# Values cast on their way in, casts of queries and keys in halves, PSUM as eight single banks, and a new order table, in a fused attention and expert-attention kernel

## The chip, the cores and the metric

The kernel runs on one core of a Trainium2 chip. The metric is the device time of one execution in microseconds (us). A core has a matrix engine (TensorE, PE in the profile, with PEld for its weight loads), three engines for element work (VectorE or DVE, ScalarE or ACT, GpSimd or POOL), a SyncE (SP) that issues transfers, and sixteen DMA engines that carry them. The engines run their own queues in order and wait for each other by semaphores. The on-chip memory is SBUF; matrix products land in PSUM, which has 128 partitions of eight banks with 512 float32 values each.

## What is computed

Two layers follow each other. The first is attention over 4 batches, 8 heads, 768 positions and 64 dimensions: each position sees the 8 first positions and the last 96, with a bias by distance whose slope depends on the head. The second takes the result as rows of 512 and runs four experts, each a causal attention with its own 64-dimensional projections; a gate picks two experts for each row and weighs them.

```python
# first layer, for each head
scores = q @ k.T / sqrt(64) - slope[h] * dist      # kept where global (first 8) or local (0 <= rel < 96)
x = softmax(scores) @ v                            # rows of all heads side by side: [4, 768, 512]
# second layer
logits = x @ w_gate                                # top 2 of 4, softmax over the two: w
for e in range(4):
    a = softmax(causal((x @ wq[e]) @ (x @ wk[e]).T / sqrt(64)))
    out += w[e] * (a @ (x @ wv[e])) @ wo[e]
```

All inputs and the output are float32; inside, the matrices are float16 and sums are float32.

## The kernel before

The work is cut into 24 units, u = 0 to 23: 4 batches of 6 row tiles of 128 positions. `unit` (from line 548) defines the operations of one unit, and each operation has a short name that the prediction and the order table use.

- Loads: `ldq`, `ldk` (line 578) bring two units of queries and keys at a time, 512 KB each, issued by SP; `ldv` (line 609) brings the values of one unit, 256 KB in runs of 256 bytes, into the ring `rawv`.
- Casts to float16: `cq`, `ck` (lines 582 and 584) for two units at once, `cv` (line 611) for the values, into the ring `V1`. All are `copy` (line 384), on POOL except for the first q and k.
- `tq`, `tk` transpose on PE; `eq`, `ek` copy the results from PSUM on DVE.
- Local attention, in two halves of four heads (hf = 0, 1): `s0`, `s1` are score products (line 630), `x0`, `x1` the exponentials on ACT (line 634), `m0`, `m1` the multiplication with a mask and distance factor `M` on DVE (line 639), `z0`, `z1` the products with the values (lines 647 and 650), which also give the row sums, `r` the reciprocals (line 661) and `n` the normalization (line 663). `kp` and `vp` put the 8 global keys and values in front of the next tiles (POOL, and a small transfer on SP).
- `tx`, `ex` transpose the rows; `pq` and `pv` (lines 689, 695) project to the experts' queries and keys, and to values and gate; `eqk`, `ev` copy them out on ACT or DVE; `xr`, `mx`, `wr`, `zi` do the gate.
- Expert attention: `s20`, `s21`, `s22` (line 727), exponentials `x20` to `x22` on ACT (line 731), the causal cut `af` on POOL (line 739), the products `y2` (line 751), then `rz`, `cw`, `n2` on DVE (lines 757 to 761), the transpose `tz`, its copy `ez`, the output product `po` (line 774), its copy `eo` on ACT or DVE, and the store `so` on SP.

No scheduler arranges this. The table `ORDER` (line 21) lists all operations in one sequence; `Stream.run` (line 328) walks through it and emits each, so every engine's queue has its operations in the table's order. A star behind a name takes the second of the engines that the operation allows, and a number after a colon names the PSUM slot. The costs that stand beside the operations (such as `{"DVE": 0.34}`) were used to make the table; at run time only the names of the engines matter. The names in the lists behind them are what must come earlier in the table.

PSUM is cut into two slots of two banks ("s", for scores) and four slots of one bank ("w", for everything else):

```python
def wtile(shape, dt, name):
    return psum.tile(shape, dt, name=name, tag=f"w{st.slots[0]}")

def stile(shape, name):
    return psum.tile(shape, F32, name=name, tag=f"s{st.slots[0]}")
```

At the start, `warm` (line 489) runs 24 products of zeros on PE. Constants are made meanwhile: `iota`, `d`, `dg`, `mask`, `d0`, `d1` on POOL and DVE, and from them the factors `M` on ACT; the weights come by `ld-q`, `ld-k`, `ld-v`, `ld-g`, `ld-o` and are cast by `w-q` and so on. At the end, `good0` to `good2` (lines 794 and 795) test that all sums are in range, `total` adds the result up and `flag` stores it; a branch to a general path follows, which isn't taken here.

Of the kernel before, what the change touches and what calls it, by code (L numbers as in the profile page):

```python
# [19 lines left out]

ORDER = """
ident nil ldq-0 warm:2 ldk-0 ident32 ldq-2 dg ldk-2 iota d mask ldv-0 d0 d1 M-1-1 ldq-4 cq-0 ck-0
ld-k M-0-0 M-1-0 tk-0:3 cq-2 tq-0:1 ek-0 ld-q M-0-1 V1one* eq-0 tq-2:2 perm kg-0 s0-0:1 ldv-1 eq-2
s1-0:0 ck-2 x0-0 x1-0 m0-0 kp-0 V2one ld-g s0-1:1 m1-0 s1-1:0 tk-2:3 x1-1 kp-1 cv-0 ek-2 vg-0 z1-0:2
x0-1 r1-0 s0-2:0 n1-0 cq-4 z0-0:0 x0-2 r0-0 vp-0 m1-1 tq-4:1 ld-v m0-2 n0-0 eq-4 ldk-4 tx-0:0 w-q*
s1-2:1 ldv-2 kp-2 w-k* cv-1 w-g ex-0 z1-1:1 m0-1 x1-2 r1-1 z0-1:3 pq-0:0 m1-2 vp-1 w-v* ldv-3 r0-1
n1-1 s1-3:1 ldq-6 n0-1 x1-3 eqk-0 tx-1:3 pv-0:2 ld-o ck-4 s20-0:0 xr-0 mx-0 s0-3:1 ex-1 x20-0 ev-0*
x0-3 wr-0 cv-2 tk-4:3 kp-3 z0-2:0 ek-4 af-0 zi-0 m0-3 y2-0:2 z1-2:1 s0-4:0 cv-3 vp-2 r1-2 r0-2
s1-4:1 rz-0 x0-4 ldk-6 pv-1:3 cw-0 kp-4 n2-0 ldq-8 n0-2 pq-1:2 x1-4 cq-6 n1-2 ldv-6 ones mx-1 ldk-8
m1-3 eqk-1* tq-6:1 tx-2:0 m1-4 w-o z0-3:2 ex-2 s20-1:1 r0-3 s0-5:0 m0-4 pq-2:0 xr-1 x0-5 wr-1 eq-6  # L30
ck-6 ev-1 n0-3 s1-5:0 eqk-2* z1-3:2 x20-1 vp-3 m0-5 tk-6:1 ldv-4 r1-3 tz-0:0 x1-5 pv-2:3 ldk-10 ek-6
af-1 n1-3 kg-6 s0-6:1 s1-6:0 ez-0 x0-6 m1-5 tx-3:2 po-0:0 x1-6 ldq-10 kp-6 m0-6 y2-1:1 ldq-12 xr-2
eo-0 cq-8 ex-3 s21-2:1 s0-7:0 rz-1 x21-2 mx-2 pq-3:2 zi-1 ldv-7 cw-1 x0-7 cv-6 ev-2* wr-2 tq-8:0
ck-8 n2-1 eqk-3* s1-7:1 eq-8 s20-2:0 x1-7 z0-6:1 tz-1:3 m1-6 tk-8:2 cv-4 r0-6 ez-1 x20-2 z1-6:0 n0-6
s20-3:1 vg-6 r1-6 z1-4:1 n1-6 po-1:3 ck-10 vp-6 ek-8 ldv-5 s21-3:0 eo-1 r1-4 tx-6:0 n1-4 pv-3:2
x20-3 kp-7 ex-6 z0-4:3 m0-7 tk-10:1 xr-3 ev-3 vp-4 cq-10 pq-6:0 r0-4 x21-3 n0-4 ek-10 tx-4:3 af-2
zi-2 ldk-12 mx-3 s0-8:1 ex-4 s1-8:0 cq-12 ldq-14 x0-8 eqk-6 pq-4:3 m1-7 so-1 tq-12:1 eqk-4* cv-7
wr-3 tq-10:0 eq-12 x1-8 s21-4:1 eq-10 cv-5 z0-7:1 z1-7:2 x21-4 r0-7 kp-8 s20-4:0 m1-8 vp-7 z0-5:0
ldv-8 z1-5:3 x20-4 r1-7 n0-7 s22-4:1 r0-5 n1-7 y2-2:1 ck-12 r1-5 x22-4 n0-5 tx-7:2 ldk-14 n1-5
s1-9:0 s20-6:1 rz-2 tx-5:3 x20-6 cw-2 ldv-9 ex-7 tk-12:0 ldq-16 x1-9 ex-5 cq-14 s0-9:1 ek-12 pq-5:2  # L40
x0-9 zi-3 n2-2 kp-9 af-4 pv-5:3 eqk-5* m0-8 s0-10:1 tq-14:1 xr-5 af-3 mx-5 x0-10 wr-5 pq-7:2 cv-8
eq-14 ev-5 m1-9 s21-5:0 eqk-7* s1-10:1 m0-10 z1-8:3 x21-5 z0-8:1 kp-10 r1-8 tz-2:2 kg-12 y2-3:0
ck-14 r0-8 vp-8 ez-2 x1-10 n1-8 ldv-10 pv-4:2 rz-3 n0-8 ldk-16 po-2:3 cw-3 ldv-12 cv-9 tx-8:1 n2-3
eo-2 s22-5:0 so-0 ex-8 s1-11:1 xr-4 ev-4 m0-9 tz-3:0 tk-14:3 x22-5 cq-16 mx-4 pq-8:1 ez-3 ek-14
x1-11 m1-10 s1-12:0 po-3:0 x1-12 af-6 eqk-8 z1-9:3 eo-3 s0-12:1 m1-12 s20-5:0 x0-12 wr-4 z0-9:1
pv-6:0 ck-16 zi-4 x20-5 r1-9 vp-9 r0-9 n1-9 y2-4:2 ldq-18 zi-5 n0-9 xr-6 so-2 ev-6 s21-8:1 rz-4
s0-11:0 af-5 mx-6 ldk-18 x21-8 wr-6 tx-9:3 tq-16:1 cw-4 ldv-11 x0-11 kp-12 ex-9 cv-10 tk-16:0 n2-4
eq-16 s20-8:1 ldv-13 s20-7:0 x20-8 m1-11 tz-4:2 pq-9:3 ez-4 ek-16 x20-7 af-8 z0-10:1 po-4:2 m0-11
eqk-9* y2-5:0 cq-18 r0-10 eo-4 n0-10 s1-13:1 rz-5 s21-9:0 cw-5 x1-13 cv-12 z1-10:1 n2-5 tq-18:2
vp-10 r1-10 m0-12 tz-5:3 x21-9 z1-12:0 ldq-20 n1-10 s0-13:1 ez-5 so-3 pv-7:1 kp-13 eq-18 ck-18 x0-13  # L50
ldk-20 po-5:3 r1-12 mx-7 ev-7* tx-10:2 xr-7 s1-14:0 zi-6 eo-5 wr-7 s0-14:1 vg-12 x1-14 zi-7 z0-12:1
ex-10 tk-18:3 af-7 vp-12 r0-12 n1-12 pq-10:2 so-5 cv-11 x0-14 ek-18 so-4 m1-13 s20-9:0 eqk-10*
z0-11:0 kg-18 n0-12 cv-13 pv-8:3 x20-9 r0-11 n0-11 tx-12:1 kp-14 z1-11:2 cq-20 mx-8 ex-12 y2-6:0
ldv-14 xr-8 s21-10:1 ev-8 rz-6 r1-11 s0-15:0 wr-8 x21-10 n1-11 y2-7:1 pq-12:3 rz-7 cw-6 cw-7 x0-15
n2-6 n2-7 tx-11:2 tq-20:0 m0-13 eqk-12* tz-7:1 s22-10:1 ex-11 s1-15:0 x22-10 ez-7 z1-13:3 kp-15
eq-20 z0-13:2 ck-20 x1-15 tz-6:1 vp-13 s1-16:1 r1-13 ez-6 n1-13 pq-11:0 ldv-15 x1-16 m0-14 ldq-22
ldv-16 po-7:1 cv-14 r0-13 eqk-11* n0-13 po-6:3 m1-14 eo-7 s21-11:0 s22-11:1 eo-6* x21-11 pv-9:1
m0-15 tx-13:2 so-6 z0-14:0 x22-11 mx-9 s0-16:0 r0-14 ex-13 pv-10:3 kp-16 n0-14 af-9 xr-9 x0-16
z1-14:2 wr-9 y2-8:0 ev-10* cv-15 vp-14 s20-10:1 r1-14 mx-10 ev-9 ldk-22 zi-8 n1-14 s1-17:0 xr-10
x20-10 ldv-19 zi-9 tk-20:1 rz-8 wr-10 so-7 cw-8 pq-13:2 m1-15 x1-17 af-10 n2-8 y2-9:3 ek-20 cq-22  # L60
eqk-13* tz-8:0 s20-11:0 ez-8 s1-18:1 rz-9 x20-11 tx-14:1 cw-9 cv-16 po-8:0 ex-14 z0-15:2 n2-9 x1-18
z1-15:1 r0-15 ck-22 tz-9:3 n0-15 eo-8 vp-15 s20-12:0 s0-17:1 r1-15 ez-9 pq-14:2 n1-15 so-8 x0-17
zi-10 m1-16 ldv-18 tq-22:3 x20-12 m0-16 po-9:0 eqk-14* m1-18 tk-22:1 eq-22 eo-9 s0-18:0 s20-13:1
m1-17 so-9 x0-18 z0-16:2 pv-11:3 ldv-17 x20-13 kp-18 ek-22 af-12 y2-10:0 mx-11 r0-16 xr-11 ev-11
cv-18 s21-14:0 wr-11 s20-14:1 x21-14 n0-16 tx-15:1 vg-18 ldv-22 z1-16:3 rz-10 x20-14 ex-15 s1-19:0
vp-16 r1-16 cw-10 pv-12:2 n1-16 x1-19 n2-10 s0-19:1 mx-12 m0-18 tx-16:3 tz-10:0 kp-19 pq-15:1 x0-19
m0-17 ez-10 ex-16 ev-12 s1-20:0 xr-12 eqk-15 s0-20:1 x1-20 po-10:0 kp-20 m1-19 z0-18:3 pq-16:1 cv-17
# [245 lines left out]
class Stream:  # L313
# [4 lines left out]
    def __init__(self, kinds):  # L318
        self.kinds = {k: [()] * n for k, n in kinds.items()}
        self.ops, self.slots = {}, []  # L320
# [27 lines left out]
def kernel(  # L348
# [37 lines left out]
    eng = {"DVE": dve, "POOL": pool}  # L386


    R = 4

# [469 lines left out]
```

## Time and profile before

| what | before |
| --- | --- |
| time, median of three runs | 146.72 us (145.56 to 147.25) |
| the profiled execution's own time | 146.58 us |
| span of the profiled execution, first to last instruction | 144.9 us |
| mean granted PE clock | 0.964 |
| packets of the DMA engines | 55,725, 27.83 MB, 72.2% of sixteen engines' span on SP's queue |
| HBM read and written | 20.98 MB, 6.29 MB |
| POOL casts of q and k | 11 each, 1,059 and 1,388 ns on average |
| SP's issue of a value load | median 537 ns, 390 to 2,152 |

A profile page gives the busy time of each engine; the span in 40 equal slices, each digit the busy tenths (for the clock, tenths of full speed); and the costliest groups, with their line, engine, what they write and read, shape and count, then busy us and mean ns of one, and after a second bar the time that the engine sat idle ahead of them and what ended it. A line 384 is the helper `copy`, so such groups are told apart by what they write. A timeline row gives start and length in us, then the same names. In a stretch of the span each engine's busy us is followed by its number of instructions in brackets.

### The profile page before, as it was taken

The numbers are of one execution on the slowest core, as the hardware profiler recorded it, in microseconds if no ns is written. First come the engines' busy times: TensorE is split into PE (matmuls) and PEld (weight loads), VectorE is DVE, ScalarE is ACT, GpSimd is POOL, SyncE is SP. The second block draws the span as 40 slices with busy tenths as digits, with TensorE's granted clock in tenths as the row PEclk, the third lists the DMA queues.
The fourth block names the chain that finished last, engine by engine and source line by source line (L and its number), as shares of the span: only waits on it lengthen the run. The fifth ranks groups of instructions, "written<-read, shape, count | busy, mean of one in ns | idle before, by whom it ended". The sixth has DMA issues, their size and how long they took to land.

```text
span 144.9 us, 5515 instructions
## 1 busy us (share of the span) xinstructions
PE 130.0 (90%) x2222; PEld 101.5 (70%) x2222; DVE 120.2 (83%) x420; ACT 120.1 (83%) x198; POOL 70.2 (48%) x116
## 2 busy tenths in 40 slices
PE   6985779697998999999999999889999999999870
PEld 2453466485877788778798787668878887978620
DVE  1257784897999989999999998989999998887870
ACT  3867766679985998988999998889999998899760
POOL 6058216534997596674773345545641370413100
PEclk9999555999999999999999999999999999999999
DMA  2999999599898997969999699770527204023164
GB/s 78 304 275 305 245 310 222 177 299 246 226 289 181 294 273 166 246 147 299 202 258 303 148 253 261 212 175 9 157 67 219 73 14 152 5 75 113 34 235 140
DMA packets 55725, 27.83 MB, mean 192 GB/s; under 512 B 26096, under 2 KB 52368, under 8 KB 55696
## 3 DMA queue, kind: packets, MB, share of 16 engines
q1 hardware_dynamic: 55696, 27.45, 72.2%
q8 instruction: 18, 0.29, 0.9%
q14 instruction: 11, 0.09, 0.2%
HBM read 20.98 MB, written 6.29 MB: 188 GB/s over the span
## 4 chain that ended last, share of the span: by engine, by line
PE 60%; DVE 14%; DMA 8%; SPq 7%; issue 3%; ACT 2%; POOL 2%; ACTq 0%
PE pq L689 13%; PE s L727 7%; PE sc L630 7%; PE pv L695 6%; PE z L647 5%; PE z L751 5%; DMA wg<-in_moe_w_gate_dram 5%; PE po L774 4%; SPq L578 4%; DMA rawqk<-in_k_dram 4%; PE tx L679 3%; PE tk L596 3%; DVE A L639 3%; PE z L650 3%; PE tq L591 3%
## 5 line engine op out<-in xcount | busy, mean ns | idle before, releaser
L634 ACT ACTIVATE A<-sc 128x1024 f16<-128x1024 f32 (+1 forms) x48 | 44.6, 960 | 6.7 <-PE sc L630 6.3
L731 ACT ACTIVATE A<-s 128x1024 f16<-128x1024 f32 (+1 forms) x48 | 43.4, 930 | 2.1 <-PE s L727 1.8
L639 DVE TENSOR_TENSOR A<-A,M 128x1024 f16<-128x1024 f16 (+1 forms) x48 | 35.0, 742 | 0.2 <-ACT A L634 0.2
L739 POOL TENSOR_SCALAR_AFFINE_SELECT A<-A 128x512 f16<-128x512 f16 x24 | 18.0, 761 | 19.6 <-ACT A L731 14.1
L689 PE MATMUL pq<-xT,wqk 128*128 128x128 f16 x384 | 26.3, 223 | 1.3 <-DVE z L761 1.2
L689 PEld LDWEIGHTS <-wqk 128*128 128x128 f16 x384 | 23.1, 100 | 2.3 <-DVE z L761 1.5
L384 POOL CAST k<-rawqk 128x1024 f16<-128x1024 f32 x11 | 15.3, 1388 | 12.7 <-DMA rawqk<-in_k_dram 12.6
L663 DVE TENSOR_TENSOR x<-z,rall 128x256 f16<-128x256 f32 x48 | 19.5, 413 | 0.4
L630 PE MATMUL sc<-qT,kT 64*128 64x128 f16 x352 | 17.4, 224 | 2.5 <-DVE kT L384 1.2
L647 PE MATMUL z<-V,A 128*128 128x65 f16 x192 | 17.1, 196 | 2.2 <-POOL V L384 1.0
L384 POOL CAST V<-rawv 128x512 f16<-128x512 f32 x24 | 15.7, 658 | 3.9 <-PE s L727 1.9
L647 PEld LDWEIGHTS <-A 128*128 128x128 f16 x192 | 13.1, 99 | 5.1 <-DVE wr L712 0.8
L727 PE MATMUL s<-QK 64*128 64x128 f16 x336 | 15.9, 219 | 0.0
L384 POOL COPY kT<-KG 128x32 f16<-128x32 f16 x20 | 5.4, 272 | 20.9 <-PE sc L630 20.9
L695 PE MATMUL pv<-wvg,xT 128*128 128x264 f16 x96 | 15.3, 283 | 0.0
L630 PEld LDWEIGHTS <-kT 64*128 64x128 f16 x352 | 11.1, 97 | 5.9 <-issue 1.9
L384 POOL CAST q<-rawqk 128x1024 f16<-128x1024 f32 x11 | 11.7, 1059 | 6.7 <-DMA rawqk<-in_q_dram 6.7
L650 PE MATMUL z<-V,A 128*128 128x65 f16 x160 | 14.6, 195 | 0.0
L384 ACT CAST QK<-pq 128x512 f16<-128x512 f32 x20 | 11.9, 595 | 2.5 <-PE pq L689 2.5
L774 PE MATMUL po<-wo,zT 128*128 128x512 f16 x48 | 13.9, 380 | 0.0
L751 PE MATMUL z<-V,A 128*128 128x65 f16 x336 | 13.8, 193 | 0.0
L751 PEld LDWEIGHTS <-A 128*128 128x128 f16 x336 | 12.3, 97 | 1.8 <-issue 0.4
(70 smaller groups left out, 226.0 us busy)
## 6 DMA issues: line engine op xcount, KB each, us to landing
rawqk<-in_q_dram SPq DMA_DIRECT2D x12, 512.0 KB
rawqk<-in_k_dram SPq DMA_DIRECT2D x12, 512.0 KB
rawv<-in_v_dram SPq DMA_DIRECT2D x24, 256.0 KB
out_dram<-o_sb SPq DMA_DIRECT2D x24, 256.0 KB
w<-in_moe_wk_dram SPq DMA_DIRECT2D x1, 512.0 KB
w<-in_moe_wq_dram SPq DMA_DIRECT2D x1, 512.0 KB
w<-in_moe_wv_dram SPq DMA_DIRECT2D x1, 512.0 KB
wo<-in_moe_wo_dram SPq DMA_DIRECT2D x1, 512.0 KB
```

The source lines that it names most:

```text
L384: act.copy(o, i) if e == "ACT" else (dve if e == "DVE" else pool).tensor_copy(o, i)
L630: mm(sc[:, par, pr, prev * P:(prev + 1) * P], lhsT=share(kT, u - prev)[L, p, :], rhs=share(qT, u)[L, p, :], start=True, stop=True)
L634: act.activation(A1[(2 * u + hf) % (2 * R)][:, :, :, 0:w], T.pop(("s", u, hf))[:, :, :, 0:w], func=Exp, scale=scale1)
L639: eng[e].tensor_tensor(a, a, M[:, hf, :, :, :] if ri else M0[:, hf, :, :, :], op=Alu.mult)
L647: mm(z[:, h % 4, :], lhsT=a[:, par, pr, 0:P], rhs=V1[i][:, h, 0:DV], start=True, stop=not ri)
L663: add(f"n{hf}", lambda e, hf=hf, r1=r1: dve.tensor_tensor(x16[i][:, 256 * hf:256 * hf + 256].rearrange("p (h d) -> p h d", d=Dh), T.pop((" ...
L689: mm(ps[:, j, :], lhsT=wqk[:, ko, j, :], rhs=xT[i][:, ko, :], start=(ko == 0), stop=(ko == nko - 1))
L695: mm(ps[:, :], lhsT=xT[i][:, ko, :], rhs=wvg[:, ko, :], start=(ko == 0), stop=(ko == nko - 1))
L727: mm(sc[:, par, n, :], lhsT=QK2[b % 2][L, ki, 2 + p2, :], rhs=QK2[b % 2][L, ri, p2, :], start=True, stop=True)
L731: act.activation(A2[i][:, :, 4 * ch:4 * ch + m, :], T.pop(("s2", u, ch))[:, :, 0:m, :], func=Exp, scale=scale2)
L751: mm(z[:, ex, :], lhsT=A2[i][:, ex % 2, n, :], rhs=V2[b % 2][:, ki, ex, 0:DV], start=(j == 0), stop=(j == len(mine) - 1))
L774: mm(ps[:, :], lhsT=zT[i][:, p2, :], rhs=wo[:, p2, :], start=(p2 == 0), stop=(p2 == E // 2 - 1))
```

## The change

The values no longer go through a float32 ring and a cast. GpSimd issues their transfer itself, and the transfer casts to float16 on the way into `V1`, whose ring grows from four to eight. The casts of queries and keys are each two instructions of half the size. PSUM is one tensor of eight banks; an operation takes any bank (`one`) or two neighbours (`two`), and the table names them. The products with the values of both halves go to two neighbouring banks and are one operation `z`, followed by one `r` and one `n` over both banks. Small products of zeros (`busy`) can be put ahead of an operation, by a number after a plus in the table: 3 before `tk-0`, 10 before `s1-0`, 1 before `s0-1`, 7 before `tk-2`, 8 before `z-1` and 9 before `tx-1`, 38 in all. The casts of `wk` and `wv` go to POOL and that of `wq` to DVE. The final check takes units 0 to 19 and 20 to 23 apart. The order table is new throughout, and with it the number of `eqk`, `ev` and `eo` on DVE: 8, 8 and 3, where there were 4, 7 and 5.

```diff
 ORDER = """
-ident nil ldq-0 warm:2 ldk-0 ident32 ldq-2 dg ldk-2 iota d mask ldv-0 d0 d1 M-1-1 ldq-4 cq-0 ck-0
-ld-k M-0-0 M-1-0 tk-0:3 cq-2 tq-0:1 ek-0 ld-q M-0-1 V1one* eq-0 tq-2:2 perm kg-0 s0-0:1 ldv-1 eq-2
...
-po-21:3 eo-20 n2-23 ez-22 tz-23:1 eo-21 good1 so-20 po-22:2 ez-23 good2 po-23:0 so-21 eo-22 good0
-eo-23 so-22 total:1 so-23 flag hint
+V1one* ldq-0 nil ident warm:0 ldk-0 ldq-2 ldv-3 dg ident32 ldv-0 iota ldk-2 ldv-2 d cq0-0 lv-0 cq1-0
+mask ld-q ldv-1 ck0-0 d1 perm d0 ck1-0 M-0-1 ldq-4 tk-0:0+3 lv-1 cq1-2 M-1-1 tq-0:6 ek-0 cq0-2 eq-0
+ldv-6 M-0-0 s1-0:01+10 s0-0:67 V2one* tq-2:5 x1-0 kg-0 ck1-2 x0-0 M-1-0 kp-0 m0-0 s0-1:67+1 ck0-2
...
+tz-22:4 good1 eo-21 so-20 ez-22 tz-23:4 po-22:5 so-21 ez-23 po-23:7 eo-22 eo-23* so-22 good2 so-23
+total:5 flag hint
 """
...
-    def wtile(shape, dt, name):
-        return psum.tile(shape, dt, name=name, tag=f"w{st.slots[0]}")
-
-    def stile(shape, name):
-        return psum.tile(shape, F32, name=name, tag=f"s{st.slots[0]}")
+    banks = psum.tile([P, 8, 4 * P], F32, name="banks")
+
+    def busy(t):
+
+        for n in range(st.idle):
+            mm(t[:, 0:P], lhsT=nil[:, 0:P], rhs=nil[:, 0:P], start=True, stop=True)
+
+    def one(dt=F32):
+
+        t = banks[:, st.slots[0], :]
+        busy(t)
+        return t if dt == F32 else t.bitcast(dt)
+
+    def two():
+
+        lo, hi = st.slots
+        assert hi == lo + 1
+        busy(banks[:, lo, :])
+        return banks[:, lo:hi + 1, :]
...
-    R = 4
+    R, RV = 4, 8
...
-    st = Stream({"s": 2, "w": 4})
+    st = Stream({"b": 8})
...
-               {"DVE": 1.1, "ACT": 1.1}, [("ld", n)])
+               {"DVE": 1.1, "POOL": 1.05}, [("ld", n)])
...
-            add("cq", lambda e: copy(e, q_[:, :, :, :], rq[:, 0, :, :, :].rearrange("p h j d -> p j h d")),
-                {"POOL": 0.99} if u else {"ACT": 0.95}, ["ldq", ("tq", u - 2 * RB)], port=True)
-            add("ck", lambda e: copy(e, k_[:, :, :, :].rearrange("p h d j -> p h j d"), rq[:, 1, :, :, :]),
-                {"POOL": 1.27} if u else {"DVE": 0.75}, ["ldk", ("tk", u - 2 * RB)], port=True)
+            for n in range(2):
+                add(f"cq{n}", lambda e, n=n: copy(e, q_[:, n, :, :], rq[:, 0, :, n, :]),
+                    {"POOL": 0.52} if u else {"ACT": 0.49}, ["ldq", ("tq", u - 2 * RB)], port=True)
+                hs = slice(4 * n, 4 * n + 4)
+                add(f"ck{n}", lambda e, hs=hs: copy(e, k_[:, hs, :, :].rearrange("p h d j -> p h j d"),
+                                                    rq[:, 1, hs, :, :]),
+                    {"POOL": 0.66} if u else {"DVE": 0.4}, ["ldk", ("tk", u - 2 * RB)], port=True)
...
-        add("ldv", lambda e: nc.sync.dma_start(rawv[i][:, :, :], v[b, :, rows, :].rearrange("h s d -> s h d")),
-            {"DMA": 1.3}, [("cv", u - R)])
-        add("cv", lambda e: copy(e, V1[i][:, :, 0:Dh], rawv[i][:, :, :]), {"POOL": 0.57},
-            ["ldv", c("V1one")] + [(n, u - R + a) for a in range(2) for n in ("z0", "z1")])
+        add("ldv", lambda e: pool.dma_start(V1[u % RV][:, :, 0:Dh], v[b, :, rows, :].rearrange("h s d -> s h d")),
+            {"POOL": 0.89}, [c("V1one")] + [("z", u - RV + a) for a in range(2)])
+        add("lv", lambda e: None, {"DMA": 1.35}, ["ldv"])
...
-            def z1(e, hf=hf):
-                a = A1[(2 * u + hf) % (2 * R)]
-                T["z", u, hf] = z = wtile([P, 4, DV], F32, "z1")
...
+        def z1(e):
+            T["z", u] = z = two()[:, :, 0:4 * DV].rearrange("l f (h d) -> l f h d", d=DV)
+            for h in range(H):
+                a = A1[(2 * u + h // 4) % (2 * R)][:, h % 2, h // 2 % 2, :]
+                mm(z[:, h // 4, h % 4, :], lhsT=a[:, 0:P], rhs=V1[u % RV][:, h, 0:DV], start=True, stop=not ri)
+                if ri:
+                    mm(z[:, h // 4, h % 4, :], lhsT=a[:, P:2 * P], rhs=V1[(u - 1) % RV][:, h, 0:DV],
+                       start=False, stop=True)
...
-            add(f"r{hf}", lambda e, hf=hf, r1=r1: dve.reciprocal(r1, T["z", u, hf][:, :, Dh]), {"DVE": 0.09},
-                [f"z{hf}"])
-            add(f"n{hf}", lambda e, hf=hf, r1=r1: dve.tensor_tensor(
-                x16[i][:, 256 * hf:256 * hf + 256].rearrange("p (h d) -> p h d", d=Dh),
-                T.pop(("z", u, hf))[:, :, 0:Dh], r1.unsqueeze(2).to_broadcast([P, 4, Dh]), op=Alu.mult),
-                {"DVE": 0.34}, [f"r{hf}", ("tx", u - R)])
+        add("r", lambda e: dve.reciprocal(r1, T["z", u][:, :, :, Dh]), {"DVE": 0.11}, ["z"])
+        add("n", lambda e: dve.tensor_tensor(
+            x16[i][:, :].rearrange("p (f h d) -> p f h d", f=2, d=Dh), T.pop(("z", u))[:, :, :, 0:Dh],
+            r1.unsqueeze(3).to_broadcast([P, 2, 4, Dh]), op=Alu.mult), {"DVE": 0.61}, ["r", ("tx", u - R)])
...
-    last = NU - 1
-    flat = rall[:, 0:last, :].rearrange("p u n -> p (u n)")
...
+    last, n0 = NU - 1, NU - 4
+    for n, (lo, hi) in enumerate(((0, n0), (n0, NU))):
+        st.add(f"good{2 * n}", inside(rall[:, lo:hi, :].rearrange("p u n -> p (u n)"), (hi - lo) * (H + E),
+                                      1.0 / SUM_HI, 1.0 / SUM_LO, 2 * n), {"DVE": (0.65, 0.4)[n]},
+               [("rz", u) for u in range(lo, hi)] + [("r", u) for u in range(lo, hi)])
```

The many other lines of the diff only put `one()` or `two()` where `wtile` or `stile` stood, put `z`, `r` and `n` where their two halves were named, and alter costs that aren't used at run time.

## The prediction

> **What bounds the kernel now.** I read the busy times first, then the 40 slices with the clock, then stretches of the span, then the rows of the costliest groups, and last the waits.
>
> ```profile
> PE 130.0 (90%) x2222; PEld 101.5 (70%) x2222; DVE 120.2 (83%) x420; ACT 120.1 (83%) x198; POOL 70.2 (48%) x116
> ...
> PEclk9999555999999999999999999999999999999999
> ...
> 15.00:27.00 12.00, 9.74 (x120) 7.56 (x120) 8.41 (x23) 7.48 (x10) 4.31 (x8) 0.57 1.01 265
> 27.00:30.00 3.00, 1.82 (x29) 1.47 (x26) 2.93 (x11) 1.91 (x3) 1.19 (x2) 1.00 0.48 135
> 30.00:130.00 100.00, 97.35 (x1837) 79.90 (x1835) 93.44 (x324) 92.35 (x148) 54.92 (x78) 1.00 0.73 185
> 130.00:145.00 15.00, 9.91 (x162) 6.66 (x158) 8.95 (x50) 8.80 (x18) 1.86 (x3) 0.99 0.37 136
> ```
>
> A stretch gives its length, then the busy us of PE, PEld, DVE, ACT and POOL, the clock, and the DMA share. From 30 to 130 us three engines are busy together (97, 93 and 92 of 100). PE's figure is not its capacity: by the pieces of the chain of waits one unit costs PE pq 0.89, pv 0.45, po 0.43, tx 0.22, local scores 2 x 0.22, local values 0.48, half of tq and tk 0.45, and on average 0.38 + 0.42 for the expert scores and values and about 0.12 for tz: 4.3 us, 103 us for 24 units. DVE and ACT, 120 us each, are the capacity. PE, in order, couples them. Before 30 us the kernel starts badly: for some 12 us the clock is near half, and all sixteen DMA engines are busy. The last 15 us are a thinning tail.
>
> ```profile
> L639 DVE TENSOR_TENSOR A<-A,M 128x1024 f16<-128x1024 f16 x40 | 31.5, 797 | 0.0
> L663 DVE TENSOR_TENSOR x<-z,rall 128x256 f16<-128x256 f32 x48 | 19.5, 413 | 0.4
> L384 POOL CAST V<-rawv 128x512 f16<-128x512 f32 x24 | 15.7, 658 | 3.9 <-PE s L727 1.9 <-DMA rawv<-in_v_dram 0.9 <-issue 0.5
> L661 DVE RECIPROCAL rall<-z 128x4 f32<-128x4 f32 x48 | 7.8, 171 | 0.5 <-PE z L647 0.2
> ...
> 105.45 0.61 POOL L384 CAST V<-rawv 128x512 f16<-128x512 f32 x1 [1.88 <-PE s L727]
> ...
> 105.53 1.08 DVE L639 TENSOR_TENSOR A<-A,M 128x1024 f16<-128x1024 f16 x1
> 106.95 0.66 DVE L639 TENSOR_TENSOR A<-A,M 128x1024 f16<-128x1024 f16 x1
> ...
> ACT A L634 <- PE sc L630: 6.3, 7, 1.3
> ```
>
> The mask multiplication takes 0.66 us alone but 797 ns on average: the one at 105.53 overlaps a POOL cast that ends at 106.06, and ends 0.55 us after it. Over 40 of them the excess is 40 x (0.797 - 0.66) = 5.5 us of DVE. The last line says how little ACT waits for scores: 6.3 us, of which 2.1 fall after 30 us.
>
> **What the Trainium skill says.** (1) "SBUF — State Buffer", Who interferes with whom: a VectorE instruction with two SBUF inputs contends with a GpSimd instruction that reads SBUF, not with one that only writes; the second to start blocks. The two rows at 105 us agree. (2) "TensorE: Matmul & The Clock Gate", Part 1: after a window of some 3.4 us with too little work the array runs at half clock. The slices at 5, after a stretch with PE at 3.05 of 5 us (15 to 20 us), agree in kind. (3) "DMA: Bandwidth & Descriptors", SWDGE vs HWDGE vs iDMA: a transfer that casts must be issued from GpSimd, whose cores write its descriptors; all queues share the same sixteen engines. No run here shows such a transfer yet.
>
> **The change part by part.** Durations are of one execution with a span of 144.9 and a time of 146.58 us, 1.7 us around the span; the median of the three runs is 146.72, so the two stand level. Where instructions of DVE or ACT follow each other, the next starts 0.07 to 0.10 us before the row's duration is over (two multiplications merged in 1.28, two n in 0.74, two exponentials in 1.94); I price by that step.
>
> *DVE, n and r.* 48 n at 0.335 = 16.1 go; 24 of 512 columns come. The row of that size from PSUM (QK from pq, 682 ns) steps by 0.60: 14.4. Gain 1.7. 48 r at 0.09 = 4.3 become 24 at about 0.10: gain 1.9.
>
> *DVE and ACT, who copies.* By the new table eqk goes 4 -> 8 times to DVE, ev 7 -> 8, eo 5 -> 3; the cast of wq moves to DVE, those of wk and wv to POOL. DVE: 4 x 0.60 + 0.33 - 2 x 0.60 + 0.7 (as the k cast of 770 ns) = +2.2. ACT: -4 x 0.49 - 0.28 + 2 x 0.49 - 3 x 0.92 = -4.0, but 2.8 of it are weight casts before 22 us, where ACT sat waiting for weights; on the path it is worth 1.3.
>
> *DVE, blocked by POOL.* 24 value casts go (15.7 of POOL's 70.2 us), and casts of 1.04 and 1.34 us become two of about half, so one block is shorter. Of 5.5 us excess I take 2 back; bounds 0 and 4. The DVE forms that would hold GpSimd off while it writes descriptors are copies with both ends in SBUF; after the start there is none.
>
> So DVE has 120.2 - 1.7 - 1.9 + 2.2 - 2 = 116.8, ACT about 116. With DVE and ACT as full as now the body shortens by the mean of DVE's 4.1 (without the wq cast) and ACT's 1.3: **2.7 us**.
>
> *POOL.* Minus 15.7, plus 22 extra starts at about 0.06 = 1.3, plus two weight casts at 1.05 = 2.1, plus 24 descriptor writings. Nothing before shows one. Below: SP's issue of the same transfer, median 0.54 us. Above no row helps: a transfer has 1,024 short rows (128 partitions by 8 heads), and at 3.4 ns a row it would be 3.5, which is rival D. I take 1.0, the first-byte figure of the skill's DMA page for this path (Specifications): an estimate. POOL comes to 82 of 145 us. Behind each writing stand the casts of q and k, the copies of global keys and the masking select (L739) that y2 waits for; POOL idles 14.1 us before that select until ACT is done, and that covers a microsecond. Behind a writing that waits for z of eight units earlier stands the same queue; a ring of eight makes that early.
>
> *DMA.* The same 24,576 rows of 256 bytes are read and half as much is written: I take no change. Below, a gain in share if the written bytes count, which ends nothing after the start, since the casts' waits for q and k there are POOL's, and POOL idles. Above, twice the values' part (6.3 of 27.5 MB, so 16 points of a 72% share). After 90 us the share is under 0.61, so even that delays only the loads before; +5 us on the end at most. SP issues 24 transfers fewer (some 0.5 us each, up to 2.3 when its queue is full) and the others on SP move up.
>
> *Start.* 38 small idle matmuls keep the clock. In the chain between 19.7 and 25.7 us PE has pq 1.71, tx 0.55, pv 0.88, tk 0.79, scores 1.3; at the full-clock prices 0.89, 0.22, 0.45, 0.44, 0.66: 2.6 us less if all of it is on the path. The idle matmuls are 4 us of PE at half clock, beside waits. I take -1.5 (0 to -2.6). Against it: four value loads start before q and k of the second pair have landed; 3 x 0.26 MB at the 0.3 MB per us of the early slices is 2.6 us for whatever waits behind; the masks' iota stands behind two writings on POOL, so d0 is done at about 7.7 instead of 4.3, and the second half of the first k cast, queued behind d0 on DVE, with it (before: k cast done at 7.66). I take +1 (0 to +2.6).
>
> *PSUM as eight banks.* 2 + 4 fixed slots become any bank or aligned pair. The waits of PE for its own earlier writes go; by the instruction lists PE waits for DVE 143 times (153 before) and for ACT 127 times as before, so one large tile doesn't chain the banks together. It can win only ACT's waits for PE after 30 us: 2.1 (local scores) + 1.6 (expert scores) + 2.5 (pq). Value -1 (0 to -3).
>
> *End.* Of the final check the two passes over 276 elements (0.30 + 0.45, after the last po) shrink to 48 elements, and the last two copies of the output go to two engines instead of 1.14 us on ACT: -0.5.
>
> Sum: -2.7 - 1.5 + 1 - 1 - 0.5 = -4.7: span 140.2, time **141.9**.
>
> **The rivals.** A is this sum, 142, own range 139 to 145.
>
> B, the table uses the freedom better: 5 of ACT's 6.2 us of waits for PE after 30 us and the whole half-clock loss (2.6) go with A's other items: 144.9 - 2.7 - 2.6 - 5 + 1 - 0.5 = 135.1, time about 137. For it: the three engines are already over 92% in the body only because the order packs them. Against: PE and DVE would have to give as much.
>
> C, given back: the value loads take the full 2.6 us at the start, the clock gives 1, and the body gains only what DVE's counts give, 3.6 - 1.5 (n and r, less the copies): -2.1 + 2.6 - 1 - 0.5 = -1: 145.6. For it: the DMA share of 1 before 27 us. Against it: PE's waits there are for masks and casts too.
>
> D, slower: POOL becomes the bound by writing descriptors. POOL was busy 62.6 us in the first 115, the stretch that holds nearly all loads. Without 23 value casts (15), with the additions (3.4) it is 51; (115 - 51)/23 = 2.8 us for each writing is the point from which it decides. At 3.5 it is 51 + 24 x 3.5 = 135 before the last values are there, and the last unit's z stood 17.5 us before the end (127.4 of 144.9): 152.5, time 154. For it: each transfer is 1,024 short rows; against it: the 1 us.
>
> That the change doesn't do what it says (banks tied together) I hold for excluded by the counted waits.
>
> **How the numbers follow.** A 0.50, B 0.17, C 0.12, D 0.21. Time: A's, 142. Range 137 to 150: below it half of B or less, above it most of D, together about 2 in 10. The three runs span 145.56 to 147.25, so about 1% (1.5 us) can be told from no change. Faster by more: A, B and a little of C, 0.68. Within: most of C, 0.09. Slower: D and the rest of C, 0.23.
>
> **What would show it.** POOL's busy sum near 82 and its transfers near 1 us each (D: over 2.8); the mean of the 128x1024 multiplication under 797 ns, near 0.74; 24 rows n near 0.68 us; the clock's slices 4 to 6 at 9; DVE near 117 with over 93% from 30 us on; SP's first weights landing no later than 18 us. I am wrong if DVE's busy sum falls and the span doesn't (a wait on values or on POOL's select took its place), or if the first pq comes after 22 us.

## The result: slower, and the profile after

| | median, us | runs | ratio to before, 95% interval |
| --- | --- | --- | --- |
| before | 146.95 | 145.56 to 147.25 | |
| changed | 153.81 | 152.94 to 158.03 | 1.048 [1.040, 1.057] |
| changed, run again (a_same) | 155.09 | 153.01 to 155.59 | 1.051 [1.038, 1.064] |

The lines below are of an execution at 155.3 us (a_same), since the one profiled first, at 158.0, lay above all others of the changed kernel. First the busy times and the clock's row, then stretches of the span, as shown of the kernel before, then rows of the costliest groups with their shapes kept apart, then three waits (us in all, times, longest).

```profile
PE 131.1 (85%) x2260; PEld 103.2 (67%) x2260; DVE 120.8 (79%) x375; ACT 116.8 (76%) x193; POOL 80.0 (52%) x146
...
PEclk9998699999999999999999999999999999999996
```

```profile
15.00:27.00 12.00, 9.17 (x145) 7.69 (x139) 6.84 (x14) 6.99 (x8) 7.47 (x13) 0.88 1.48 228
27.00:30.00 3.00, 2.36 (x51) 1.88 (x52) 2.25 (x6) 1.91 (x3) 1.40 (x4) 1.00 0.73 176
30.00:130.00 100.00, 92.35 (x1710) 75.65 (x1708) 92.67 (x279) 86.28 (x139) 56.87 (x92) 1.00 0.82 159
130.00:154.00 24.00, 16.63 (x290) 12.35 (x287) 14.20 (x66) 14.06 (x24) 3.44 (x5) 0.94 0.27 102
```

```profile
L658 DVE TENSOR_TENSOR A<-A,M 128x1024 f16<-128x1024 f16 x40 | 32.2, 814 | 0.0
L629 POOL DMA_DIRECT2D V<-in_v_dram x24 | 21.4, 891 | 1.6 <-PE banks L671 1.5
L678 DVE TENSOR_TENSOR x<-banks,rall 128x512 f16<-128x512 f32 x24 | 16.5, 686 | 0.4
...
L677 DVE RECIPROCAL rall<-banks 128x8 f32<-128x8 f32 x24 | 4.8, 200 | 2.2 <-PE banks L671 1.6 <-ACT V L400 0.2 <-PE banks L669 0.2
```

```profile
POOL A L753 <- ACT A L745: 31.0, 10, 5.9
...
DVE kT L400 <- PE banks L615: 7.2, 4, 3.7
ACT QK L400 <- PE banks L703: 4.6, 5, 2.2
```

The sizes of the parts are as expected: n 686 ns, r 200, a transfer 0.89 us of POOL, POOL's sum 80. But DVE is no less busy than before (120.8 beside 120.2; in the execution at 158.0 it has 119.3), the mask multiplication's mean has not come near 740 ns (814 beside 797; at 158.0 it is 786), and from 30 to 130 us PE does 92.35 us of work beside 97.35 and ACT 86.28 beside 92.35. That work comes later: from 130 us on PE still has 16.6 us to do, where it had 9.9. DVE waits 7.2 us for the transposed keys, where it waited 2.7. POOL waits 31 us for ACT ahead of its select, where it waited 14; ahead of the copies of the global keys it waits 10.2 us, where it waited 20.9. In all POOL stands idle for 73 us, and for 75 before: the waits have moved.

### The profile page after: what moved, and what is told of

It reads as the page before. It is cut to its first block, busy times and chain, and to the rows that moved or that the text cites. A ratio compares the mean times of both kernels' runs of the same rounds, so it can differ in the third digit from the quotient of the medians.

```text
span 156.3 us, 5620 instructions
## 1 busy us (share of the span) xinstructions
PE 134.7 (86%) x2260; PEld 105.7 (68%) x2260; DVE 119.3 (76%) x375; ACT 116.4 (74%) x193; POOL 79.1 (51%) x146
## 3 DMA queue, kind: packets, MB, share of 16 engines
q0 software_dynamic: 24960, 3.15, 31.6%
## 4 chain that ended last, share of the span: by engine, by line
PE 54%; DMA 16%; DVE 10%; ACT 6%; POOL 5%; issue 4%; SPq 2%; DVEq 0%; ACTq 0%; POOLq 0%
PE banks L703 9%; DMA rawqk<-in_k_dram 9%; PE banks L741 6%; PE banks L765 6%; PE banks L709 5%; DMA rawqk<-in_q_dram 5%; PE banks L649 5%; PE banks L788 4%; PE banks L669 4%; ACT A L745 4%; PE banks L615 3%; PE banks L693 3%; PE banks L671 3%; PE banks L610 2%; DVE A L658 2%
## 5 line engine op out<-in xcount | busy, mean ns | idle before, releaser
L745 ACT ACTIVATE A<-banks 128x1024 f16<-128x1024 f32 (+1 forms) x48 | 42.9, 927 | 11.3 <-PE banks L741 10.3
L653 ACT ACTIVATE A<-banks 128x1024 f16<-128x1024 f32 (+1 forms) x48 | 44.5, 961 | 6.6 <-PE banks L649 5.9
L703 PE MATMUL banks<-xT,wqk 128*128 128x128 f16 x384 | 25.5, 219 | 0.1
L629 POOL DMA_DIRECT2D V<-in_v_dram x24 | 21.3, 889 | 1.3 <-PE banks L671 1.1
L649 PE MATMUL banks<-qT,kT 64*128 64x128 f16 x352 | 17.0, 226 | 2.8 <-POOL kT L400 2.0
L400 POOL CAST k<-rawqk 128x512 f16<-128x512 f32 x22 | 16.5, 774 | 5.7 <-DMA rawqk<-in_k_dram 5.6
L669 PE MATMUL banks<-V,A 128*128 128x65 f16 x192 | 15.5, 200 | 3.3 <-DVE z L775 2.2
L678 DVE TENSOR_TENSOR x<-banks,rall 128x512 f16<-128x512 f32 x24 | 16.5, 686 | 0.4
L741 PE MATMUL banks<-QK 64*128 64x128 f16 x336 | 16.5, 221 | 0.2 <-ACT A L653 0.2
L709 PE MATMUL banks<-wvg,xT 128*128 128x264 f16 x96 | 15.1, 289 | 0.0
L788 PE MATMUL banks<-wo,zT 128*128 128x512 f16 x48 | 14.4, 391 | 0.0
L765 PE MATMUL banks<-V,A 128*128 128x65 f16 x336 | 14.0, 193 | 0.1
L671 PE MATMUL banks<-V,A 128*128 128x65 f16 x160 | 13.3, 198 | 0.3 <-DMA V<-VG 0.2
```

The source lines that it names most:

```text
L400: act.copy(o, i) if e == "ACT" else (dve if e == "DVE" else pool).tensor_copy(o, i)
L629: add("ldv", lambda e: pool.dma_start(V1[u % RV][:, :, 0:Dh], v[b, :, rows, :].rearrange("h s d -> s h d")), {"POOL": 0.89}, [c("V1one")] ...
L649: mm(sc[:, par, pr, prev * P:(prev + 1) * P], lhsT=share(kT, u - prev)[L, p, :], rhs=share(qT, u)[L, p, :], start=True, stop=True)
L653: act.activation(A1[(2 * u + hf) % (2 * R)][:, :, :, 0:w], T.pop(("s", u, hf))[:, :, :, 0:w], func=Exp, scale=scale1)
L669: mm(z[:, h // 4, h % 4, :], lhsT=a[:, 0:P], rhs=V1[u % RV][:, h, 0:DV], start=True, stop=not ri)
L671: mm(z[:, h // 4, h % 4, :], lhsT=a[:, P:2 * P], rhs=V1[(u - 1) % RV][:, h, 0:DV], start=False, stop=True)
```

## The experiments

Each run stood beside the kernel before on the same chip; I compare ratios to it. Runs with b alter the kernel before, runs with a the changed kernel. The expectations name three theories. T, transfer time: a row that is cast on its way keeps the DMA engines longer. S, the start: loads stand behind the small transfer vp-0 on SP, and PE starts late. Q, the queue: a writing of descriptors on POOL delays what stands behind it there.

### The transfers of the values

**b_cast_dma**: the kernel before with the casting transfers on POOL and what they need, a ring of eight and its column of ones written first.

```diff
-        add("ldv", lambda e: nc.sync.dma_start(rawv[i][:, :, :], ...
-        add("cv", lambda e: copy(e, V1[i][:, :, 0:Dh], rawv[i][:, :, :]), {"POOL": 0.57},
+        add("ldv", lambda e: pool.dma_start(V1[u % RV][:, :, 0:Dh], ...
```

> The kernel before, its old table, with one part of the change alone: the values come by GpSimd's casting transfers into a ring of eight, and the value casts on GpSimd are gone. T: slower than before by most of the change's loss, 150 to 154 us. S, or any fault of the new table: no slower than before, 144 to 147, since GpSimd has less to do and SP has 24 issues less.

150.6 us, 1.026 [1.017, 1.034]: the transfers alone cost about half of the loss. The table of DMA queues (packets, MB, share of sixteen engines) seemed to give the reason: 24,960 packets at 32 ns each (0.330 x 151.5 us x 16 / 24,960). A plain row of 256 bytes took 19.7 ns: SP's queue carries 24,960 packets fewer and is busy (0.722 x 144.9 - 0.488 x 151.5) x 16 = 491 us less. These are times of packets and not of engines: in the changed kernel their sum is 1.48 of sixteen engines' time from 15 to 27 us, so packets overlap in time, and what a row costs by itself may be less than 32 ns.

```profile
q1 hardware_dynamic: 30736, 21.15, 48.8%
q0 software_dynamic: 24960, 3.15, 33.0%
```

**a_values_8**: the changed kernel without the transfers of units 8 to 23, whose values are then those of earlier units. **a_pool_plain**: POOL issues plain float32 transfers and casts them. **a_sp_values**: SP issues plain loads, POOL casts.

```diff
-        add("ldv", lambda e: pool.dma_start(V1[u % RV][:, :, 0:Dh], ...
-        add("lv", lambda e: None, {"DMA": 1.35}, ["ldv"])
+        add("ldv", lambda e: nc.sync.dma_start(rawv[u % RV][:, :, :], ...     # a_pool_plain: pool.dma_start
+        add("lv", lambda e: copy(e, V1[u % RV][:, :, 0:Dh], rawv[u % RV][:, :, :]), {"POOL": 0.57},
```

> The changed kernel without the value transfers of units 8 to 23; those units use the values that units 0 to 7 left, so the sums go on but the output differs. It takes 16 of 24 transfers, some 33 us of sixteen engines, and 14 us of GpSimd away, and leaves the start as it is. T: 142 to 147. S: 150 or more, since the start is unchanged and carries the loss.

> The changed kernel with the value transfers still issued by GpSimd in the same places, but plain (float32, 256-byte rows on both ends) into a float32 ring of eight, and GpSimd casts them, some ten places ahead of their first use in the table. T: row time back to about 20 ns and 144 to 149 us, although GpSimd has 15.7 us more to do. S: 152 or more, since the table stays.

> The changed kernel with its first part undone: SP issues plain float32 loads of the values into a ring of eight, POOL casts them ten places ahead of their first use, and the eight first loads stand later, about where the kernel before has them; all else (halved casts, banks, z, idle products, table) as changed. Theory T (DMA time of the cast rows): the loads take about 72 points of share again, not 80, and the time is 4 to 5 us under the changed kernel unaltered, 150 to 151.5. If writing the transfers on POOL was a large part too (it holds DVE's mask multiplications): 147 to 150. If POOL's casts of values at places that the table did not provide cost as much as they save: 153 to 158.

149.9 us, 1.020 [1.009, 1.030]; 160.1, 1.090 [1.077, 1.102]; 151.3, 1.029 [1.021, 1.036]. By the ratios, 3 to 5 us come back without 16 transfers or with SP's loads (a_values_8 lies between what the two theories gave); with plain transfers, which the DMA engines carry in 1,920 packets and 16.5% of share, the kernel gets 5 to 6 us slower still, though POOL also has 24 casts more there. a_pool_plain and a_sp_values have the same casts and differ in who issues, and in the places of the first loads: 160.1 and 151.3. That spoke against DMA time. So the two were set apart in the old order.

**b_pool_plain**: the kernel before, its plain loads issued by POOL at the same places of the table. **b_dma_extra**: the kernel before with one more plain load behind each, from SP, into a tile that nobody reads.

```diff
-        add("ldv", lambda e: nc.sync.dma_start(rawv[i][:, :, :], ...
+        add("ldv", lambda e: pool.dma_start(rawv[u % 8][:, :, :], ...          # b_pool_plain
+        add("ex2", lambda e: nc.sync.dma_start(spare[i][:, :, :], v[b, :, ri * P:ri * P + 88, :]...   # b_dma_extra
```

> The kernel before with one thing changed: the value loads are issued by POOL at the same places of the table, plain, from and to float32, into a ring of eight; POOL casts them as before. POOL gains 24 x 0.9 = 21.6 us, near 91; the DMA time of these rows falls (16 points of share in the changed kernel with plain transfers by POOL, where SP's took 21). Theory T (the cast rows' DMA time made the casting transfers slow): no slower than before by over 1%, 145 to 148. Theory Q (the issue's place in POOL's queue, ahead of casts that PE waits for, made them slow): as slow as the casting ones, or slower, since POOL is fuller: 150 to 153.

> The kernel before with one cost added and nothing else: behind each load of values SP issues one more of 704 rows of 256 bytes into a tile that nobody reads, 704 x 19.6 ns = 13.8 us of engine time, which is what a transfer of 1,040 cast rows took beyond a plain one (1,040 x 32.3 - 1,024 x 19.6 = 13.5 us). Theory T: 3 to 5 us slower than before, 149 to 151, as the casting transfers alone did (150.6). If those were slow by POOL's writing or by what it does to DVE, and not by the DMA engines: within 1.5 us of before, under 148.

b_pool_plain: 154.4 us, 1.054 [1.046, 1.062]. The DMA engines have less to do than before (their table below: 66% of 152.6 us in these two queues; before, 72.2% of 144.9 on SP's), and the loss is larger than with casting. It is POOL's issuing that costs, with the casts still there. One way shows in the timeline, POOL's rows first and then some of DVE's (start, length, then the names; rows of one engine overlap by up to 0.1 us):

```profile
q1 hardware_dynamic: 30736, 21.15, 49.1%
q0 software_dynamic: 1920, 6.29, 16.9%
```

```profile
43.80 0.88 POOL L609 DMA_DIRECT2D rawv<-in_v_dram  x1
44.67 0.51 POOL L384 COPY kT<-KG 128x32 f16<-128x32 f16 x1
45.13 1.03 POOL L384 CAST q<-rawqk 128x1024 f16<-128x1024 f32 x1
46.13 0.63 POOL L739 TENSOR_SCALAR_AFFINE_SELECT A<-A 128x512 f16<-128x512 f16 x1
46.72 1.03 POOL L384 CAST q<-rawqk 128x1024 f16<-128x1024 f32 x1
47.70 1.16 POOL L384 CAST V<-rawv 128x512 f16<-128x512 f32 x2
48.81 0.66 POOL L384 COPY kT<-KG 128x32 f16<-128x32 f16 x1
49.42 0.90 POOL L609 DMA_DIRECT2D rawv<-in_v_dram  x1
```

```profile
44.31 0.81 DVE L639 TENSOR_TENSOR A<-A,M 128x1024 f16<-128x1024 f16 x1
...
47.25 2.15 DVE L639 TENSOR_TENSOR A<-A,M 128x1024 f16<-128x1024 f16 x1
```

POOL has no gap. A multiplication that comes to stand beside its casts waits through a cast of q, two of V and a copy, and ends at 49.40, when the last of them has (49.47): 2.15 us for 0.66. In the same stretch of the kernel before, POOL had gaps of 0.3 to 1.6 us. A writing alone seldom holds it: in b_cast_dma six multiplications stand beside writings and nothing else, five at 0.68 us and one, beside two writings in a row, at 0.95. The writings fill POOL's gaps, and DVE's busy sum is 123.9 us, 3.7 more than before. That this is the whole of the 8 us is not shown.

Such places are found in the changed kernel too, here with halved casts. DVE's multiplication, cw and the next multiplication take 4.7 us for 1.5:

```profile
50.91 1.18 POOL L400 CAST q<-rawqk 128x512 f16<-128x512 f32 x2
52.02 0.88 POOL L629 DMA_DIRECT2D V<-in_v_dram  x1
52.91 0.66 POOL L753 TENSOR_SCALAR_AFFINE_SELECT A<-A 128x512 f16<-128x512 f16 x1
53.49 0.62 POOL L400 CAST q<-rawqk 128x512 f16<-128x512 f32 x1
```

```profile
51.56 1.08 DVE L658 TENSOR_TENSOR A<-A,M 128x1024 f16<-128x1024 f16 x1
52.56 1.58 DVE L772 SCALAR_TENSOR_TENSOR cw<-wr,zi,rall 128x4 f32<-128x4 f32 x1
54.06 2.06 DVE L658 TENSOR_TENSOR A<-A,M 128x1024 f16<-128x1024 f16 x1
```

b_dma_extra missed what both theories gave: 166.2 us, 19.7 above the kernel before, nearly the whole length of what was added (24 x 13.8 / 16 = 20.7 us). SP's issues took up to 2.8 us each, and small transfers and loads of q and k stood behind the new ones in SP's queue. It shows that SP's queue, or the DMA engines behind it (before, their share is 0.95 over the first 90 us), had no slack; it does not price rows in another queue, as it was meant to.

**b_place**, **a_place**: b_cast_dma and the changed kernel, 19 transfers of each moved in the table to where POOL idled.

```diff
-... ldv-12 ... kp-10 ...
+... ldv-10 ldv-11 ldv-12 kp-10 ...
```

> The kernel before with casting transfers alone (150.6), of which 19 now stand in POOL's queue just ahead of an instruction before which POOL idled 0.8 us or more in that run's profile, some up to 18 us sooner or later than they stood, none nearer than 8 us to its first use. Theory Q by place (a transfer's 0.9 us delays the casts and selects behind it): the loss of 4 us shrinks to 2 or less, 146.5 to 148.5. Theory T (DMA time of cast rows): the rows are the same, no change, 150 to 152. If being on POOL at all costs (it holds DVE wherever it stands): 149.5 to 151.

> The changed kernel (155.1) with the same edit: 19 of its transfers moved to where POOL idled in its profile, most of them later. Theory Q by place: 149 to 152.5. Theory T or a cost wherever they stand: 154 to 156. If the later transfers make values late (z waits for their landing, 6.5 us after issue): over 156.

150.4 us, 1.031 [1.021, 1.041], and 152.3, 1.042 [1.034, 1.051]. In the old order nothing can be told of place: two of b_place's four executions (148.6 and 149.7) lie below b_cast_dma's (149.8 to 150.8, and one at 153.2), two (151.2 and 151.8) do not. In the new order it is worth perhaps 1 us, with intervals that overlap.

So issuing by POOL costs in b_pool_plain, but whether the 4 us of the casting transfers are POOL's queue, the cast rows' DMA time, or both, stays open. DVE's blocked time does not show in it: in b_cast_dma and b_place DVE's busy sum is 119.9 and 119.4 us and the multiplication's mean 761 and 758 ns, none above before. The chain of waits that ended last in b_cast_dma's profile (an execution at 153.2) has something of both theories. At 37.79 us a writing of 0.84 us stands between a cast of q and a cast of k that PE waits for; and the last load of k, issued at 87.89, takes 7.25 us, where before the same load, issued at 85.40, took 5.57.

### The other parts, each in the old order

**b_split**: the casts of q and k halved. **b_banks**: PSUM as eight banks, banks chosen anew. **b_zrn**: as b_banks, with z, r and n merged at the place of the later half, and one z moved up by a few places. **b_idle**: 51 idle products. **b_end**: the end alone. **b_all**: casting transfers, halved casts, banks and merged z together.

```diff
-... z1-0:2 x0-1 r1-0 s0-2:0 n1-0 cq-4 z0-0:0 x0-2 r0-0 ... n0-0      # b_zrn, without its new banks
+... x0-1 s0-2 cq-4 z-0 x0-2 r-0 ... n-0
-... s1-0:0 ... s0-1:1                                                # b_idle
+... s1-0:0+9 ... s0-1:1+10
-... good2 po-23:0 so-21 eo-22 good0 eo-23 so-22 total:1              # b_end
+... po-23:0 so-21 eo-22 eo-23* so-22 good2 total:1
```

> The kernel before with one part of the change alone: each cast of q and k is two instructions of half the size, one behind the other at the place of the whole. What I predicted (shorter blocks of DVE): the mean of the 128x1024 multiplication falls from 797 ns to 0.74 or less, DVE's busy sum by 2 us, time 145 to 146. If instead POOL's two instructions back to back hold DVE through both: mean unchanged or higher, time 146 to 148.

> The kernel before with PSUM as eight single banks, chosen so that each operation takes a bank that was given back long ago; z, r and n stay in halves, order, values and casts as before. It is the control to the run with z, r and n merged (152.4). My term: 0 to 3 us gain, 143.5 to 146.5. If banks or their choice made the merged run slow: 150 or more. If it was the merging, which moves the first half of z, n behind the second: 144 to 147.5 here.

> The kernel before with one part alone: PSUM as eight banks, one z, r and n for both halves at the place of the later half; all else, values and casts and order too, as before. By my sum n gives 1.7 us and r 1.9 us of DVE: DVE's busy sum 116 to 117.5, and the span shortens by about half of that to all of it, time 143 to 146. If the merged z is late instead (n, tx and pq wait for the second half): DVE falls as much and the time doesn't, 146 to 149. S and T say nothing of it: values and the start are those of before.

> The kernel before with one part alone: 51 idle products of zeros ahead of s1-0, s0-1, tk-2, s0-2, z1-0, z0-0, z1-1 and z0-1, where PE waits at 10 to 20 us. My prediction's term: the clock's slices 4 to 6 go from 5 to 9 and the time falls by 1.5 us (0 to 2.6), 144 to 146.5. If the start is set by loads and casts and not by the clock, the clock rises and the time stays, 146 to 147.5.

> The kernel before with the end of the change alone: the test of the sums in units 0 to 19 ahead of the last units' work, that of 20 to 23 at the end, and the last copy of the output on DVE. My term: 0.5 us less, 145.5 to 146.5 beside 146.5. If the branch or the last store ends the time and not the test: no difference.

> All parts of the change but its order table and its choice of engines: casting transfers, halved casts, eight banks, merged z, r and n, in the order of the kernel before. If the parts make the loss and add up (4.5 + 0.4 + 1.8 + 4 us): 155 to 158, and the new table gains nothing or little over the old one. If the parts hide in each other's waits: 151 to 154. If the new table is itself to blame for half: under 151.

| run | median, us | ratio to before |
| --- | --- | --- |
| b_split | 147.3 | 1.002 [0.999, 1.005] |
| b_banks | 148.4 | 1.012 [1.007, 1.017] |
| b_zrn | 152.4 | 1.033 [1.026, 1.041] |
| b_idle | 147.1 | 0.999 [0.996, 1.002] |
| b_end | 147.9 | 1.007 [1.004, 1.010] |
| b_all | 158.5 | 1.082 [1.075, 1.090] |

No part gains. Merging costs about 2% over the banks (1.033 / 1.012): its n and r take less of DVE, but r now waits. The rows of the reciprocals, of b_zrn and then of b_banks:

```profile
L672 DVE RECIPROCAL rall<-banks 128x8 f32<-128x8 f32 x24 | 4.9, 202 | 5.3 <-PE banks L666 2.0 <-PE banks L664 1.7 <-PE banks L778 0.9
```

```profile
L680 DVE RECIPROCAL rall<-banks 128x4 f32<-128x4 f32 x48 | 7.8, 170 | 0.7 <-PE banks L669 0.2 <-PE banks L666 0.2
```

DVE saves 2.9 us on r and idles 4.6 more ahead of it, since the first half of z is done late; the gain went into a new wait. (My choice of banks differs between the two runs, so part of the 2% may be that.)

b_idle raises the clock, as these stretches show (before: 0.57 from 15 to 27 us), and the time stays:

```profile
15.00:27.00 12.00, 8.47 (x118) 6.68 (x117) 7.22 (x21) 7.44 (x9) 4.09 (x8) 0.72 0.93 239
27.00:30.00 3.00, 1.69 (x35) 1.14 (x32) 2.93 (x9) 1.94 (x2) 1.52 (x3) 1.00 0.34 123
```

In b_end's chain the two passes over 276 elements are gone, but DVE's last copy of the output (ahead of the test in its queue) ends at 141.09 of a span of 145.2, where before the test ended at 140.49 of 144.9: one wait for another, in these two executions.

The parts add up in b_all: 0.2 + 3.3 + 2.6 = 6.1% apart, 8.2% together. The new table with its choice of engines brings that down to 5.1%: it does not make the loss, it takes some of it back.

### The start

**a_start**: ld-k, ldk-4, ld-g and ld-v ahead of vp-0 on SP. **a_start_v8**: that, without the transfers of units 8 to 23 (old values stand in). **a_wact**: the casts of wk and wv on ACT.

```diff
-... z-0:01 w-q vp-0 s1-2:67 ld-k s0-2:23 m1-1 ldk-4 ... ld-g ... ld-v
+... z-0:01 w-q ld-k ldk-4 ld-g ld-v vp-0 s1-2:67 s0-2:23 m1-1
-               {"DVE": 1.1, "POOL": 1.05}, [("ld", n)])                # a_wact
+               {"DVE": 1.1, "ACT": 1.1}, [("ld", n)])
```

> The changed kernel with one thing undone: the loads ld-k, ldk-4, ld-g and ld-v stand ahead of vp-0 in the table, so that SP issues them near 8 us, when it has issued ldq-4, and not after vp-0 at 17.7 us. Theory S (the start: these loads wait behind vp-0, ldk-4 lands at 25.4 us and holds POOL's cast, tk-4 and through it the first expert scores): 3 to 6 us less than the changed kernel unaltered (155.1), 149 to 152; the k of the third pair lands before 20 us, and ACT is busy over 1.5 us in each 3 us from 24 on. Theory T (the rows of the casting transfers keep the sixteen DMA engines full, so loads that are issued earlier only land at one another's cost): at most 2 us less, 153 to 155.

> The changed kernel with the four loads ahead of vp-0, and without the value transfers of units 8 to 23 (these units use the values that their place in the ring held before, so the output is other numbers). Without the transfers alone it took 149.9. If S and T add up and are all of the loss: 144 to 147, no slower than the kernel before (146.1). If the new table has a further cost in its body (order of DVE and ACT, POOL's instructions back to back): 148 to 150.

> The changed kernel with the casts of wk and wv on ACT again, as before, and not on POOL. If POOL, which waits 3.2 us for these weights and holds the casts of the third pair behind them, makes the late start: 151 to 153.5. If not: 154 to 156 (ACT has 2.1 us more to do, at a time when it waits).

Both came out slower, where theory S had them faster: 167.3 us, 1.126 [1.114, 1.137], and 156.6, 1.061 [1.051, 1.072], beside 1.051 for the changed kernel and 1.020 for a_values_8. a_wact took 154.1, 1.054 [1.047, 1.061], no different from the changed kernel; its DVE has 117.2 us of busy time, less than a_same's 120.8, and no time came of it. The chain of a_start says why (start, length, what):

```profile
18.33 7.67 DMA V<-VG
26.00 0.04 issue
26.04 0.21 PE banks L671
```

The transfer of eight rows, 8 KB, takes 7.67 us, behind the loads of weights and keys that were now issued ahead of it, and z of the next unit waits for it. The table has vp-0 ahead of them for this; the price is that SP stands from 9.1 to 17.7 us in the changed kernel, waiting for z-0, and the third pair's keys land at 25.4. The edit undid one wait and made a longer one, so it neither shows nor refutes that the late start costs time.

**a_same**, the changed kernel unaltered, gave the profile above.

> The changed kernel once more, unaltered, for an undisturbed profile. Theory T (transfer time: a row cast on its way takes the DMA engines 32 ns where a plain one took 20, so loads fill nearly all of the first 115 us): 152 to 155 us, software queue near 49 us of sixteen engines. Rival S (the new table puts two weight loads and k of the third pair behind the key copy vp-0 on SP, and PE starts late): the same time, with the first pq well after 24 us and a stall near 27 us.

## Why the prediction was wrong

Forecast: 142 us, range 137 to 150; measured 153.8. Two steps failed.

The first is in *DVE and ACT*: "With DVE and ACT as full as now the body shortens by the mean of DVE's 4.1 (without the wq cast) and ACT's 1.3". It took the two engines for the capacity, so that time taken from them would come off the span. a_sp_values has what I forecast for them, DVE 116.3 and ACT 117.0 where I had 116.8 and about 116, and none of the casting transfers:

```profile
PE 133.3 (89%) x2260; PEld 104.3 (70%) x2260; DVE 116.3 (78%) x375; ACT 117.0 (78%) x193; POOL 75.9 (51%) x146
```

It takes 151.3 us, 2.9% more than before and 9 us more than the forecast, so most of the miss stands without the casting transfers (in part it may be the value casts on POOL, for which that table had no places). In place of the gain came waits: DVE stands idle for 33 us of that span, where it had 25. It waits for PE 6.7 us ahead of the transposed keys (2.7 before) and 4.1 us ahead of r (before, r idled 0.5 us in all). The second of these comes by itself in b_zrn: DVE has 118.4 us, 1.8 less than before, and the time grows by 3.3%. That a merged z makes r and n wait for the second half was not in the working at all; the 4.6 us of new idle time ahead of r there are more than the 3.6 that n and r were to bring. In the changed kernel r idles 2.2 us, so the new order leaves part of it.

The second is *POOL*: "POOL idles 14.1 us before that select until ACT is done, and that covers a microsecond." The size was right (1.0 taken, 0.89 measured; sum 82 taken, 80 measured). The cover was not: with the casting transfers alone POOL has 5 us more to do (75.3) and the time grows by 2.6% (b_cast_dma); with nothing but the writings added it grows by 5.4% (b_pool_plain). Of the 75 us that POOL idled before, these 14.1 lie in five waits, and in the stretches shown the writings stand elsewhere, between casts and copies. That this is the reason is not shown, since no gain could be told from b_place, where 19 writings stand where POOL idled; how much is the queue and how much slower loads stays open.

Point by point:

- *DVE, blocked by POOL*: -2 us taken with bounds 0 and 4. The means can't price it: the changed kernel has 814 and 786 ns in two executions and 728 in a_wact, and kernels with the old casts have from 753 (b_idle) to 813 (b_banks). In b_split the mean is 761 and DVE has 1.6 us less, near what I took, and the time stays (1.002). What was wrong is the picture of one multiplication blocked by one cast: without gaps one is blocked through several POOL instructions.
- *DVE, n and r*: n came as sized (0.68 taken, 686 ns); the rows of r, half as many, grew from 171 to 200 ns.
- *DMA*: "I take no change" was wrong in the row: the casting queue's packets take 32.4% of the changed kernel's span, where the values' took about 21% before (491 us of 16 x 144.9). Whether that costs time isn't settled.
- *Start*: the clock did rise (one slice at 8 and one at 6, where three were at 5), and b_idle prices that at nothing in the old order: -0.7 to +0.2 us, where I took -1.5. (The stretch from 15 to 20 us with PE at 3.05 of 5 does not stand ahead of the slow slices, as I read it, but in them; from 10 to 15 us PE has 3.09 of 5 at full clock.) For the loads in front I took +1, but the first pq, with my own mark at 22 us, came at 23.6 (before: 20.2). "The others on SP move up" failed: four loads stand behind vp-0. How much of the 5% the start makes, no run isolates.
- *PSUM as eight banks*, -1: by itself 0.7 to 1.7% slower with my banks; in the changed kernel ACT's waits for PE on queries and keys grew from 2.5 to 4.6 us.
- *End*, -0.5: 0.4 to 1.0% slower by itself.

Rival D's number, 154 us, came out by luck: it needed over 2.8 us for each writing, and one took 0.89; POOL is busy 52% of the span and is not the bound.

The skill's page "SBUF — State Buffer" (Who interferes with whom) describes the ports that VectorE and GpSimd share as an exclusive lock, held in the two-port modes for the whole instruction, and I counted one instruction. The trace has 2.15 us through four. Its page "Perfetto Trace Analysis" (DMA Instruction — SWDGE (GPSIMD)) says that such a row ends when the descriptors are written, not when the data are there; here 0.89 us of row and 6.5 us from issue to landing agree.

## What to carry to other kernels

Busy time taken from the busiest engines is not time taken from the span. Here three engines are busy over 90% in lockstep, and kernels with 2 to 4 us less of DVE (b_zrn, a_wact, a_sp_values) were no faster; ask which wait ends last, and what the change adds to it. Merging two operations to save their fixed cost can lose more by the wait of the first half.

An engine's idle sum does not say that new work is free: POOL idled half of the span, and 21 us of writings on it still cost 5.4% in b_pool_plain. Do one part of such a change at a time in the old order first; here no part gained anything by itself.

## What was unexpected in the hardware

A plain transfer of 1,024 rows of 256 bytes went in 80 packets when POOL issued it (1,920 / 24) and took 17% of share; issued by SP or cast, it went in 1,040, about one for each row. A writing on POOL took 0.89 to 0.91 us either way, and with one exception DVE's multiplication beside it took no longer (0.68 us). A transfer of 8 KB took 7.67 us behind large loads in SP's queue.
